# Regions of rows per expert, paced loads and a new order of the attention in a sketched-attention and hash-routed expert kernel

## The chip, the cores and the metric

The kernel runs on one core of a Trainium2 chip. A core has five engines with a queue of instructions each: PE (matrix multiplications; its weight loads are listed apart as PEld), DVE (vector), ACT (scalar), POOL (general) and SP (here only an issuer of DMAs). Each runs its own queue strictly in order, and semaphores between them make one wait for another. DMAs are issued from the queues of SP, ACT and POOL. The metric is the device time of one execution in microseconds.

## The reference

Attention by a sketched polynomial kernel, then a layer of experts chosen by a hash of the token's number:

```python
batch, n_heads, seq, head_dim = (4, 4, 1088, 32); r = 8
def phi(x):
    a = np.einsum('rd,bhsd->bhsr', S1, x)
    b = np.einsum('rd,bhsd->bhsr', S2, x)
    return np.einsum('bhsi,bhsj->bhsij', a, b).reshape(*x.shape[:-1], r * r)
q_p, k_p = (phi(q), phi(k))
kv = np.einsum('bhsf,bhsd->bhfd', k_p, v)
z = np.sum(k_p, axis=2)
num = np.einsum('bhsf,bhfd->bhsd', q_p, kv)
den = np.einsum('bhsf,bhf->bhs', q_p, z)[..., None] + 1e-06
attn = num / den                          # (B, H, S, D) -> x of (B*S, H*D) = (4352, 128)

expert_idx = token_ids * np.int64(2654435761) % np.int64(8)
for e in range(8):                        # w1: (8, 128, 1024), w2: (8, 1024, 128)
    out[expert_idx == e] = np.maximum(x[expert_idx == e] @ w1[e], 0.0) @ w2[e]
```

## The kernel before

Everything is computed in 32-bit floats. The order of the instructions on each engine is written out by hand: the program's order is the order of each engine's queue.

**Attention.** It goes batch by batch (`b` from 0 to 3). A batch has 1024 main rows, held as 128 partitions by 8 rows, and 64 tail rows; the tails of two batches share one tile of 128 partitions. For the main rows of a batch PE transposes k (`turned`, 8 transposes; ACT copies them out of PSUM in two `kT` tiles) and multiplies by the sketch (`side_ab`, 32 small matmuls to a bank `abk`). `first_copied` has ACT copy the first factor, and DVE multiplies the two to 64 features a row (`main_features`, two operations of 128x1024 a side). q goes the same way, but DVE transposes it in blocks of 32x32 (`q_blocks`, two operations), so that its rows come out in another order within blocks of 32. `parted_features`, used for batch 0, gives the second half of a tile to POOL. `kv_products` (64 matmuls, and 8 for the tail) builds kv and, by a column of ones in the tile `va` (`values`), z; `kv_diagonal` copies it out (`m`). `f_turned` has PE transpose the features of q (16 transposes, four copies by ACT), `x_products` multiplies them by `m` in three chunks, and `normalized` has DVE divide by the denominators into the tile `xs`. `keep_busy` is idle matmul work that fills PE's waits near the start.

**Routing.** DVE finds each token's expert (`route_experts`), a scan counts the tokens per expert along the columns (`route_scan`), PE sums the counts over partitions (`route_counts`), and experts are ordered by how many rows they have left (`route_places`, `route_order`). Rows of the first two batches are early, those of the other two late. An expert takes its first 256 early rows as an early group; what is left joins its late rows, and the expert in place r has room for 320 - 7r of those. `route_slots` turns a token's rank into a slot in one array of 35 tiles of 128 rows (16 operations on 34 columns), with a row past the end for a token that found no room; the rows that the block transposes of q have exchanged are put right by one matmul (`route_blocks`, `route_blocks_end`). POOL scatters the finished rows by an indirect DMA each (`scatter_x`, 34 of 128 rows) to `x_rows` in HBM, with the token's number beside each row. `x_rows` was filled with zeros before (L181). Since an empty slot then reads as token 0, `empty_slots` computes on DVE, during expert group 0, which slots are empty (`none`), and `name_rows` ORs this into the rows' numbers (`put`), which makes the last scatter skip them.

**Experts.** There are 16 groups, the 8 early ones of 256 columns and the 8 late ones of 320 to 271. In group g PE does the 8 parts `c` of layer 1 (L922) with those of layer 2 of the group before (L930) in between; ACT and DVE take turns in `evict`. Beside it, at places (g, c) set by `at`, SP fetches the rows of a later chunk (`fetch`, one DMA a chunk), DVE splits them into 16-bit halves and SP turns them by DMA (`turn_in`), and DVE joins the halves (`join_in`), on which layer 1 of that chunk waits. The results go back in the same way (`turn_out`, `join_out`) and are scattered to the output by POOL. Chunks 0 and 1 are turned by PE instead (`bring`). The experts' weights come in 512 KB pieces, w1 and w2: those of places 0 to 3 are issued during the attention, the other four pairs at (0, 3), (1, 3), (2, 3) and (3, 3) (`load_experts`).

**Loads.** SP's queue issues in this order: k0, q0, k1, v0, q1, the tails of k (4 DMAs), v1, the tails of v (4), k2, q2, the fill of `x_rows`, v2, the tails of q (4), k3, q3, v3, four pairs of weights, four fetches. Two tiles each of k, q and v are in turn, so a load waits till the tile two batches back is read. ACT's queue issues the token ids, the main part (L124) first and then the two tails (L127). Nothing else holds a load back.

Of the kernel before, what the change touches and what calls it, by code (L numbers as in the profile page):

```python
# [9 lines left out]
F32 = mybir.dt.float32  # L10
# [20 lines left out]
def kernel(  # L31
# [12 lines left out]
    nc = tc.nc  # L44
# [18 lines left out]
    EB = B - 2  # L63
    CE = TT * T + 1
    GE, GL, GD = 256, 320, 7
# [7 lines left out]
    XW = DM + 4  # L73
    GQ = T // Q
# [32 lines left out]
    tok = const.tile([P, C, 2], I32)  # L107
# [13 lines left out]
    def load_tok():  # L121

        ids = _words(moe_token_ids).rearrange("(b s two) -> b s two", b=B, two=2)
        nc.scalar.dma_start(tok[:, 0:B * T].rearrange("p (b t) two -> p b (t two)", b=B),  # L124
                            ids[:, 0:SM].rearrange("b (p t) two -> p b (t two)", t=T))
        for x in range(TT):
            nc.scalar.dma_start(tok[half_rows(x), B * T:], ids[x::TT, SM:].rearrange("u s two -> s u two"))  # L127

    def load_tail(src, name):

        t = const.tile([P, B // TT, H, D], F32, name=name)
        for b in range(B):
            nc.sync.dma_start(t[half_rows(b), b // TT], src[b, :, SM:, :].rearrange("h p d -> p h d"))
        return t

    def load_main(src, b, tag):
        t = load.tile([P, H, T, D], F32, tag=tag, name=f"{tag}{b}")
        rows = src[b, :, 0:SM, :].rearrange("h (p t) d -> p h t d", t=T)
        if (b, tag) != (0, "k"):
            nc.sync.dma_start(t[:], rows)  # L140
            return t
# [12 lines left out]
    def load_experts(rs, eng=nc.sync, eng_type=ENG.SP):  # L154
# [3 lines left out]
            skip_runtime_bounds_check_because="a count of the experts ahead of one of them is below their number")  # L158
        for r, e in zip(rs, es):
            eng.dma_start(w1[:, r], moe_w1[bass.ds(e, 1)].rearrange("o p f -> p (o f)"))  # L160
            eng.dma_start(w2[:, r], moe_w2[bass.ds(e, 1)].rearrange("o (c p) d -> p (o c) d", p=P))


    k_t.append(load_main(k, 0, "k"))
    load_tok()
    act = const.tile([P, 1], F32)
    nc.scalar.memzero(act[:])
    zeros = const.tile([P, XW], F32)
    nc.scalar.memzero(zeros[:])
# [6 lines left out]
    v_t.append(load_main(v, 1, "v"))  # L176
    v_tail = load_tail(v, "v_tail")
    k_t.append(load_main(k, 2, "k"))
    q_t.append(load_main(q, 2, "q"))
    x_dram = nc.dram_tensor("x_rows", (ST * P + N, XW), F32)  # L180
    nc.sync.dma_start(x_dram[0:ST * P].rearrange("(n p) d -> p n d", p=P),  # L181
                      zeros[:].unsqueeze(1).to_broadcast([P, ST, XW]))
    v_t.append(load_main(v, 2, "v"))
    q_tail = load_tail(q, "q_tail")
    k_t.append(load_main(k, 3, "k"))
    q_t.append(load_main(q, 3, "q"))
    v_t.append(load_main(v, 3, "v"))


    warm = const.tile([P, 1], BF16)  # L190
    G_.memset(warm[:], 1.0)
    ident = const.tile([P, P], F32)
    make_identity(nc, ident[:])
    own_t = const.tile([P, Q], F32)
# [40 lines left out]

    keep_busy(WARM)


    tokens = const.tile([P, C], F32)
    in_blocks = const.tile([P, B, T], F32)  # L240
    block_less = const.tile([P, 1], F32)
    second_half = const.tile([P, 1], F32)
    xs = [const.tile([P, T, XW], F32, name=f"xs{b}") for b in range(B)]
    xs_tail = [const.tile([P, XW], F32, name=f"xs_tail{u}") for u in range(B // TT)]
    first_slot = const.tile([P, 2, E], F32)
    slot_at = const.tile([P, ST], F32)
    caps_of = const.tile([P, E], F32)

    def numbers():

        for t in xs:
            G_.memset(t[:, :, DM + 1:], 0.0)
        for t in xs_tail:
            G_.memset(t[:, DM + 1:], 0.0)
        for cls in range(B // TT):
            iota_of(tokens[:, main_cols(cls)], [[S, TT], [1, T]], cls * TT * S, T)
        tails = tokens[:, T * TT::CE]
        iota_of(tails, [[TT * S, B // TT]], SM, 1)
        G_.memset(second_half[:], 0.0)
        G_.memset(second_half[P // 2:, :], float(S - SP))  # L260
        G_.tensor_tensor(tails, tails, second_half[:].to_broadcast([P, B // TT]), op=OP.add)
        for u in range(B // TT):
            G_.tensor_copy(xs_tail[u][:, DM:DM + 1].bitcast(I32), tokens[:, tail_col(u):tail_col(u) + 1])
        iota_of(in_blocks[:], [[S, B], [Q, GQ], [T * D, Q]], 0, T)
        for j in range(Q):
            G_.memset(block_less[j * D:(j + 1) * D, :], float(j * (T * D - 1)))
        G_.tensor_tensor(in_blocks[:], in_blocks[:], block_less[:].unsqueeze(2).to_broadcast([P, B, T]), op=OP.subtract)
        for b in range(B):
            G_.tensor_copy(xs[b][:, :, DM:DM + 1].bitcast(I32), in_blocks[:, b].unsqueeze(2))
        iota_of(slot_at[:], [[P, ST]], 0, 1)  # L270
        iota_of(caps_of[:], [[-GD, E]], GL)
        iota_of(first_slot[:, 0], [[GE, E]])
        for r in range(E):
            G_.memset(first_slot[:, 1, r:r + 1], float(E * GE + sum(caps[:r]) + (GAP if r == E - 1 else 0)))
# [63 lines left out]
    RB = 14  # L338
    assert N < 1 << RB - 1 and E << RB < 1 << 23
    pos = const.tile([P, C], F32)  # L340
    sidx = const.tile([P, C], I32)
    none = const.tile([P, ST], I32)
    put = const.tile([P, ST], I32)

    def route_experts():
        eid_i = const.tile([P, C], I32, name="eid_i")
        by_class = eid_i[:].rearrange("p (k c) -> p k c", c=CE)
        for lo, hi, src in ((0, TT * T, tok[:, 0:B * T, 0].rearrange("p (k c) -> p k c", k=NC)),
# [886 lines left out]
```

## Time and profile before

| | us |
|---|---|
| median of 3 runs | 195.11 |
| lowest and highest | 192.71, 195.12 |
| the profiled execution | 195.1 |
| its span, first to last instruction | 193.4 |
| first matmul of the experts (L922) | at 61.6 |
| first scatter of rows to `x_rows` | at 33.6 |
| first fetch of rows from `x_rows` issued | at 56.6 |
| last 16 matmuls of the experts (L1120) | at 186.9, 1.95 long |

A row of a timeline has the start, the duration, the engine, the line of the kernel, the operation, output and inputs, the shapes and how many instructions are merged; in brackets stands how long the engine was idle before it and what ended that. SPq and POOLq are the issuing of those engines. In a row of groups the numbers behind the count are the busy time in us and the mean of one in ns. "Issue" as a releaser means that the profile shows nothing that the engine waited for.

### The profile page before, as it was taken

The page shows a single profiled execution, that of the slowest core. Times are in us where ns is not written, and L with a number is a line of the kernel's source. Part 1 is how long each engine was busy: PE and PEld are TensorE (multiplying, and loading weights), DVE is VectorE, ACT ScalarE, POOL GpSimd, SP SyncE. Part 2 cuts the span into 40 slices and gives each one's busy share as a digit, 9 for nine tenths or more (in the row PEclk, how much of TensorE's full clock was granted, in tenths as well). Part 3 has the DMA queues.
Part 4 walks back from the last instruction along what each step waited for, and adds up shares of the span by engine and source line. Part 5 has one row for each costly group of instructions (what it writes and reads, how often), then busy time and mean ns, then how long its engine had stood idle before and what let it go on. Part 6 is the DMA issues. An engine that isn't in the chain of part 4 may idle for free. (4 is left out here: it accounts for less than half of the span.)

```text
span 193.4 us, 4148 instructions
## 1 busy us (share of the span) xinstructions
PE 173.0 (89%) x1512; PEld 141.7 (73%) x1513; DVE 106.0 (55%) x326; ACT 60.9 (31%) x156; POOL 82.4 (43%) x141
## 2 busy tenths in 40 slices
PE   7849789799487899869999999999999999999990
PEld 2637577699487687648888888777777777778990
DVE  3299999897274875143453365263344746424330
ACT  2423546444241313201332332321313313131320
POOL 7736500877777777040440341240412404144762
PEclk9987999999999999978999999999999999999999
DMA  4896999999729634996924325324223183130110
GB/s 107 272 317 170 299 236 236 363 366 365 239 63 220 202 77 94 255 287 110 261 67 93 84 66 111 73 66 97 67 55 81 40 91 90 27 95 28 40 36 28
DMA packets 48069, 28.40 MB, mean 147 GB/s; under 512 B 22116, under 2 KB 45925, under 8 KB 48048
## 3 DMA queue, kind: packets, MB, share of 16 engines
q1 hardware_dynamic: 44736, 23.43, 48.5%
q0 software_dynamic: 2208, 4.53, 7.6%
q10 hardware_dynamic: 1104, 0.17, 0.5%
q8 instruction: 12, 0.20, 0.5%
q14 instruction: 9, 0.07, 0.1%
HBM read 17.42 MB, written 6.96 MB: 126 GB/s over the span
## 5 line engine op out<-in xcount | busy, mean ns | idle before, releaser
L930 PE MATMUL op<-hT,w 128*128 128x256 f32 (+8 forms) x256 | 77.2, 392 | 0.0
L933 POOL DMA_INDIRECT out_dram<-os,put x35 | 34.0, 971 | 78.7 <-DVE put L814 48.5
L760 DVE TENSOR_SCALAR hT<-hp 128x256 f32<-128x256 f32 (+9 forms) x68 | 28.9, 427 | 56.5 <-PE hp L922 46.0
L930 PEld LDWEIGHTS op<-hT,w 128*128 128x128 f32 x256 | 48.0, 192 | 10.9
L758 ACT ACTIVATE hT<-hp 128x256 f32<-128x256 f32 (+9 forms) x68 | 26.4, 390 | 72.7 <-PE hp L922 68.5
L922 PE MATMUL hp<-xT,w 128*128 128x256 f32 x128 | 38.6, 391 | 3.9 <-issue 2.8
L922 PE MATMUL hp<-xT_late,w 128*128 128x320 f32 (+8 forms) x144 | 41.9, 385 | 0.0
L660 POOL DMA_INDIRECT x_rows<-xs,sidx x32 | 31.9, 996 | 20.0 <-DVE den L653 11.4
L922 PEld LDWEIGHTS hp<-xT,w 128*128 128x128 f32 x128 | 24.4, 194 | 8.8 <-issue 3.2
L922 PEld LDWEIGHTS hp<-xT_late,w 128*128 128x128 f32 x144 | 25.4, 190 | 6.8
L626 PE MATMUL fT_ps<-ident,f 128*128 128x128 f32 x64 | 8.4, 279 | 2.1 <-issue 1.9
L575 DVE TENSOR_TENSOR f<-first_of_ab,abq_ps 128x1024 f32<-128x1024 f32 x7 | 8.3, 1217 | 3.5 <-ACT first_of_ab L562 3.5
L833 DVE COPY xh<-xg 128x256 uint16<-128x256 uint16 (+1 forms) x28 | 9.6, 386 | 0.0
L627 ACT COPY fT<-fT_ps 128x512 f32<-128x512 f32 x16 | 8.4, 605 | 2.7 <-PE fT_ps L626 2.7
L626 PEld LDWEIGHTS fT_ps<-ident,f 128*128 128x128 f32 x64 | 6.8, 140 | 3.2 <-issue 2.4
L608 PE MATMUL kv<-va,kp 128*64 128x66 f32 x256 | 8.5, 222 | 0.3 <-ACT both_of_ab L569 0.3
L608 PEld LDWEIGHTS kv<-va,kp 128*64 128x64 f32 x256 | 8.2, 137 | 0.7 <-POOL is_at L401 0.7
L575 DVE TENSOR_TENSOR kp<-first_of_ab,abk_ps 128x1024 f32<-128x1024 f32 x7 | 8.2, 1205 | 0.8 <-ACT first_of_ab L562 0.8
L637 PE MATMUL x_ps<-m,fT 128*64 128x66 f32 x256 | 8.4, 222 | 0.0
L537 PE MATMUL abq_ps<-s_k,qT 128*64 128x64 f32 x128 | 5.6, 237 | 3.2 <-issue 3.0
L637 PEld LDWEIGHTS x_ps<-m,fT 128*64 128x64 f32 x256 | 8.0, 137 | 0.3 <-issue 0.2
L970 ACT COPY half<-op 128x256 uint16<-128x256 uint16 x16 | 5.2, 375 | 7.4 <-PE op L930 7.4
(195 smaller groups left out, 153.5 us busy)
## 6 DMA issues: line engine op xcount, KB each, us to landing
w<-in_moe_w_dram SPq DMA_DIRECT2D x16, 512.0 KB, 7.4
x_rows<-zeros SPq DMA_DIRECT2D x1, 2310.0 KB
q<-in_q_dram SPq DMA_DIRECT2D x4, 512.0 KB, 5.2
v<-in_v_dram SPq DMA_DIRECT2D x4, 512.0 KB
xg<-x_rows SPq DMA_DIRECT2D x13, 129.0 KB, 2.4
k<-in_k_dram SPq DMA_DIRECT2D x3, 512.0 KB, 4.3
xg<-x_rows SPq DMA_DIRECT2D x3, 193.5 KB, 2.6
out_dram<-os,put POOLq DMA_INDIRECT x35, 2.5
```

Of the source, the lines that this page charges most:

```text
L575: eng.tensor_tensor(dst, a[:, r].unsqueeze(3).to_broadcast(shape), ab[:, r].unsqueeze(2).to_broadcast(shape), op=OP.mult)
L608: nc.tensor.matmul(kv[HALVES[x], z], f[:, x], w.rearrange("p h d -> p (h d)"), start=(n == 0 and z == 0), stop=(n == T), skip_group_check= ...
L626: nc.tensor.transpose(p[:, j, z], f[:, (t0 + j) // Q, z, (t0 + j) % Q].rearrange("p h f -> p (h f)"), ident[:])
L627: nc.scalar.copy(fT[:, t0:t0 + 2], p[:])
L637: nc.tensor.matmul(p[x, j, z], fT[:, t0 + j, z, x], m[:, z], start=True, stop=True, skip_group_check=True)
L660: st_ = G_.indirect_dma_start(out=x_dram[:], out_offset=bass.IndirectOffsetOnAxis(ap=sidx[:, c:c + 1], axis=0), in_=row, in_offset=None, b ...
L758: nc.scalar.activation(dst, src, AF.Relu if relu else AF.Copy)
L760: return nc.vector.tensor_scalar(dst, src, 0.0, None, op0=OP.max).ins
L833: nc.vector.tensor_copy(xh[:, x * w:(x + 1) * w].rearrange("p (a b) -> p a b", a=n), xg3[k][:, 0:n].bitcast(U16).rearrange("p a (b two) -> ...
L922: nc.tensor.matmul(hp[:, 0:hi - lo], w1[:, g % E, c * P:(c + 1) * P], x_columns(first_of(g) + lo, first_of(g) + hi), start=True, stop=True)
L930: nc.tensor.matmul(ops[g][:, 0:hi - lo], w2[:, g % E, c], hTs[g][:, c, lo:hi], start=(c == 0), stop=(c == FC - 1))
L933: st_ = nc.gpsimd.indirect_dma_start(out=out[:], out_offset=bass.IndirectOffsetOnAxis(ap=idx, axis=0), in_=src, in_offset=None, bounds_che ...
```

## The change

- **Rows.** `x_rows` gets a region of 256 + 4352 rows per expert, in the experts' order. A token's row there is one sum: its place times the region's length, plus its rank among the expert's rows (`route_rows`); early rows past 256 run on into the part of the late ones. `route_bases`, `route_ranks`, `route_slots` and `empty_slots` go. The early rows' numbers are ready with `route_early`; `route_late` and the block matmul follow for the late ones, in batch 2.
- **Empty rows.** The fill writes rows whose number is too large for the output to be written (`empty_row`), in four DMAs and one for the gap, instead of zeros in one DMA; `name_rows` becomes a copy. It is issued ahead of v1.
- **Fetches.** A chunk that straddles two regions is fetched in several DMAs.
- **Batches** come in the order 0, 2, 1, 3 (`BATCH`), so that each tail tile is loaded by two DMAs instead of four. The tail of the ids has a tile of its own; one half is issued first on ACT, the other by POOL.
- **Room**: 313 - 5r instead of 320 - 7r. The sum is the same, 2364 columns.
- **Paced loads.** `pace` makes a load of SP wait until the third before it has landed. The last four pairs of weights are issued singly, at (0, 2), (0, 6) and then (g, 4) for g from 1 to 6, each after PE's latest matmul of layer 1 at that place.
- **q of the first two batches** is transposed by PE (`side_turned`) with copies by ACT, and its rows keep their order.
- **Order of the attention.** The features of q of batch 0 are all made by DVE; the value tails are copied by ACT and the k tail's features made by DVE instead of POOL. The loop is arranged so that in batch b come, in this order, kv, the transposes of q's features, the products of the next k, x, the products of the next q and the transposes of the k after, while DVE makes the features of k, normalises and then makes those of q.
- The loop for overflowing tokens at the end, which these inputs don't enter, is rewritten for the new rows.

```diff
+    BATCH = [0, 2, 1, 3]
-    GE, GL, GD = 256, 320, 7
+    GE, GL, GD = 256, 313, 5
+    XR = GE + N
...
+        tail(0, nc.scalar)
+        nc.scalar.dma_start(tok[:].rearrange("p (b t) two -> p b (t two)", b=B),
                             ids[:, 0:SM].rearrange("b (p t) two -> p b (t two)", t=T))
+        return lambda: tail(1, nc.gpsimd)
...
+    def pace(ld, ahead=3):
+        if len(paced) >= ahead:
+            tc.add_manual_dep(ld.ins, paced[-ahead].ins.name,
+                              mybir.DependencyInfo(mybir.DependencyClass.Sync, mybir.DependencyReason.DATA), reason="pace")
+        paced.append(ld)
...
-            nc.sync.dma_start(t[:], rows)
+            pace(nc.sync.dma_start(t[:], rows))
...
+        for lo, hi, p in ((0, GE, P), (GE, GE + FL, h)):
+            n = (hi - lo) // p
+            for es in (slice(0, E // 2), slice(E // 2, E)):
+                pace(nc.sync.dma_start(regions[es, lo:hi].rearrange("e (p n) d -> p e (n d)", n=n),
+                                       empty_row[0:p, 0:n].rearrange("p n d -> p (n d)").unsqueeze(1)
+                                       .to_broadcast([p, E // 2, n * XW])))
+        nc.sync.dma_start(x_dram[1 + E * XR:], empty_row[:, 0])
...
+    G_.memset(empty_row[:, :, DM:DM + 1].bitcast(I32), BIG)
+    fill_rows()
+    v_t.append(load_main(v, 1, "v"))
+    q_tail = load_tail(q, "q_tail")
...
+        nc.vector.tensor_tensor(cnt[:, 0, 1], cnt[:, 0, 1], took[:], op=OP.add)
+        nc.vector.scalar_tensor_tensor(base[:], place[:].unsqueeze(1).to_broadcast([P, NC, E]), float(XR), cnt[:, 0],
                                        op0=OP.mult, op1=OP.add)
+    def route_rows(u, dst):
+        rows = seq[:, :, u]
+        nc.vector.tensor_tensor(rows, rows, base[:, u].unsqueeze(2).to_broadcast([P, E, CE]), op=OP.add)
+        nc.vector.tensor_tensor(rows, rows, mask[:, :, u * CE:(u + 1) * CE], op=OP.mult)
+            nc.vector.tensor_reduce(dst, rows.rearrange("p e c -> p c e"), axis=AX.X, op=OP.add)
...
+    kT = side_turned(k_t[0])
     route_experts()
     route_scan()
+    same_in_blocks()
     keep_busy(2)
     abk = side_ab(kT, "abk_ps")
+    cp_of()
+    kp = parted_features(parted_copied(abk), "kp", 2)
+    number_early()
+    number_late()
+    cnt = route_counts()
+    qT = side_turned(q_t[0])
     keep_busy(3)
     va = values(0, nc.scalar.copy)
+    abq = side_ab(qT, "abq_ps", x_bank)
+    firsts = first_copied(flat(abq))
     route_places(cnt)
     route_order()
+    kT = side_turned(k_t[1])
+    f = all_features(firsts, "f", 1)
+    kTt = tail_turned(k_tail, "kTt_ps")
+    for x in range(TT):
+        nc.scalar.copy(va_tails[x][half_rows(x), :, :, 0:D], v_tail[half_rows(x)])
     kv = kv_products(0, kp, va, None, 0, T)
+    abt = tail_products(kTt, "abt_ps")
+    tail_features(kp_tail, first_copied(abt))
+    route_early()
+    fT = f_all(f)
     kv_products(0, kp, va, kv, T)
     m = kv_diagonal(0, kv)
+    abk = side_ab(kT, "abk_ps")
...
+    for b in range(1, B):
+        kv = kv_products(b, kp, va)
+        m = kv_diagonal(b, kv)
+        if b == 1:
+            qT = q_blocks(q_t[2])
+        if b == 2:
+            route_late()
+        fT = f_all(f)
...
+            abk = side_ab(kT, "abk_ps")
+            if b == 2:
+                route_blocks_end(route_blocks(x_bank))
...
+        x_ps = x_all(b)
...
+            kp = all_features(firsts, "kp", 2)
+            abq = side_ab(qT, "abq_ps")
+            firsts = first_copied(flat(abq))
+        if next2:
+            kT = side_turned(k_t[b + 2])
+        x_normalized(b, x_ps)
...
+            f = all_features(firsts, "f", 1)
...
+            lds = load_experts(range(E // 2))
+            for ld in lds[:6]:
+                pace(ld())
+            for k in range(4):
+                fetch(k)
+            for ld in lds[6:]:
+                pace(ld())
...
-    for r in range(E // 2, E):
-        at(r - E // 2, 3, load_experts, range(r, r + 1))
+        ld = later.pop(0)()
+        tc.add_manual_dep(ld.ins, last_mm[0].ins.name,
+                          mybir.DependencyInfo(mybir.DependencyClass.Sync, mybir.DependencyReason.DATA), reason="pace")
+    places = [(0, 2), (0, 6)] + [(g, 4) for g in range(1, E - 1)]
+    for i, (g, c) in enumerate(places):
+        at(g, c, load_next, None if i % 2 else E // 2 + i // 2)
```

More of the change, by code (lines that the diff above doesn't have):

```diff
@@ L247 @@
[L247 to L253, printed above, removed]
-            G_.memset(t[:, DM + 1:], 0.0)
[L255 to L274, printed above, removed]
@@ L462, in route_blocks_end @@
     def route_blocks_end(p):
-        V = nc.vector
         own = spread[:].rearrange("p (n t) i -> p n t i", t=Q)
-        V.tensor_tensor(own, p[:], own_t[:].unsqueeze(1).unsqueeze(3).to_broadcast([P, NC * TT * GQ, Q, Q]), op=OP.mult)
-        V.tensor_reduce(gap[:, 0:NC * TT * T], own.rearrange("p n t i -> p n i t"), axis=AX.X, op=OP.add)
-        for u in range(NC):
-            V.tensor_copy(sidx[:, main_cols(u)], gap[:, u * TT * T:(u + 1) * TT * T])
-    filled = const.tile([P, ST], F32)
@@ L507, in turned @@
+        nc.vector.tensor_tensor(own, p[:], own_t[:].unsqueeze(1).unsqueeze(3).to_broadcast([P, TT * GQ, Q, Q]), op=OP.mult)
+        with nc.allow_low_precision(reason="the numbers of rows are whole"):
+            nc.vector.tensor_reduce(sidx[:, main_cols(1)], own.rearrange("p n t i -> p n i t"), axis=AX.X, op=OP.add)
     def turned(src, g):
@@ new lines, in x_normalized, with x_all @@
+    def x_normalized(b, x_ps, chunks=CHUNKS):
+        for (t0, n), p in zip(chunks, x_ps):
+            normalized(xs[b][:, t0:t0 + n, 0:DM], p, n)
+            for t in range(t0, t0 + n):
+                scatter_x(xs[b][:, t], col_of(b, t))
+    def x_all(b):
+        return [x_products(fT, m, t0, n) for t0, n in CHUNKS]
+    x_ps = x_all(0)
+    qT = side_turned(q_t[1])
+    va_next = values(1, nc.scalar.copy)
+    kp_next = feature_tile(work, "kp", 2)
+    main_features(kp_next, firsts, 0)
@@ L893 @@
             scatter_tail(1)
-        if more:
-            kp, va = kp_next, va_next
-        if b == TT:
-            for k in range(4):
-                fetch(k)
     feats.release()
@@ L1047, with load_next @@
     at(0, 3, bring, 1)
[L1050 to L1052 removed]
     for k in range(4, G):
         at(k - 3, 2, fetch, k)
[L1055 to L1056 removed]
+    later = []
+    def load_next(r):
+        if r is not None:
+            later.extend(load_experts(range(r, r + 1)))
+        ld = later.pop(0)()
[4 more added lines that the diff above has]
+        at(g, c, load_next, None if i % 2 else E // 2 + i // 2)
     for k in range(G):
```

398 lines of the change are left out of this document (159 added, 239 removed).

## The prediction

> **What bounds the kernel now.** I read the page first (busy shares, the 40 slices), then stretches of the span with each engine's busy time, then the timeline where PE is not full.
>
> ```profile
> span 193.4 us, 4148 instructions
> ...
> PE 173.0 (89%) x1512; PEld 141.7 (73%) x1513; DVE 106.0 (55%) x326; ACT 60.9 (31%) x156; POOL 82.4 (43%) x141
> ...
> PE   7849789799487899869999999999999999999990
> ```
> ```profile
> 10.00:20.00 10.00, 7.40 (x138) 6.33 (x139) 9.59 (x21) 2.97 (x7) 4.90 (x7) 0.83 0.90 244
> ```
> ```profile
> 24.90:61.40 36.50, 30.97 (x738) 28.44 (x740) 27.44 (x61) 16.82 (x37) 21.32 (x22) 1.00 0.92 261
> ...
> 66.50:188.90 122.40, 119.16 (x535) 97.23 (x535) 56.48 (x199) 33.44 (x95) 41.81 (x44) 0.99 0.41 95
> ```
>
> The columns of a stretch are its length, then busy time and count of PE, weight loads, DVE, ACT, POOL, then clock, DMA share and GB/s. From 66.5 us on PE is the bound (119.2 of 122.4). Before that nothing is full for long: from 10 to 20 us DVE is (9.59 of 10), with PE's clock at 0.83; from 24.9 to 61.4 PE has 31.0 of 36.5. So the sum goes by three marks on PE: M1, the end of the transposes of batch 0's q features (25.4, the row of 24.98 below); M2, the end of the last x products (61.4); M3, the first matmul of expert group 1 (66.5).
>
> **To M1.**
>
> ```profile
> 8.36 0.17 DVE L350 TENSOR_SCALAR eid_i<-tok 128x2 int32<-128x2 int32 x1 [2.73 <-DMA tok<-in_moe_token_ids_dram]
> ...
> 9.40 2.48 DVE L356 TENSOR_TENSOR_SCAN seq<-keep,mask 128x272 f32<-128x272 f32 x1
> ...
> 12.18 0.17 PE L363 MATMUL cnt<-cp,before 128*128 128x16 bf16 x1 [2.74 <-ACT cp L360]
> ...
> 14.18 1.97 PE L511 MATMUL kT_ps<-ident,k 128*128 128x128 f32 x8
> ...
> 15.94 1.08 PE L234 MATMUL idle<-warm 128*128 128x512 bf16 x3
> ...
> 19.18 1.13 PE L537 MATMUL abk_ps<-s_k,kT 128*64 128x64 f32 x32
> ...
> 24.98 0.44 PE L626 MATMUL fT_ps<-ident,f 128*128 128x128 f32 x2 [1.69 <-issue]
> ```
> ```profile
> tok<-in_moe_token_ids_dram ACTq DMA_DIRECT2D x2, 1.0 KB, 4.3
> ```
> ```profile
> 29.11 1.09 PE L511 MATMUL kT_ps<-ident,k 128*128 128x128 f32 x8
> ```
>
> The tails of the token ids land last, and DVE waits 2.73 us for them. One now goes first on ACT, the other is issued by POOL. How soon a piece issued by POOL lands is not in the trace: with the 4.3 us of ACT's pieces, after an issue near 2 us, it gains 2.1 us, at worst nothing; I take 1.5, nearest to the same small piece. The counting matmul then runs at 10.7 instead of 12.2, and PE idles some 1.9 us before it instead of 2.74; I take it that the slow clock (8 transposes 1.97 instead of 1.09) doesn't follow. Behind it on PE stand 8 new transposes of q (1.1), three keep-busy matmuls (1.1) and the products of q (1.1): 14.0, about as now (14.18), because the q transposes take what the ids gave. From there to M1 PE needs 11.2 us today. Of these go 1.13 (32 products, now behind M1), 1.08 (the keep-busy work, now ahead), 0.9 (the slow clock) and the 1.69 of waiting: 6.4 stay, and I add 0.2 for ACT, which copies the value tails now. M1 is 20.6, 4.8 earlier; bounds 2 (the ids gain nothing, the slow clock stays) and 6 (ids 2.1, no other wait).
>
> **M1 to M2.**
>
> ```profile
> L575 DVE TENSOR_TENSOR f<-first_of_ab,abq_ps 128x1024 f32<-128x1024 f32 x7 | 8.3, 1217 | 3.5 <-ACT first_of_ab L562 3.5
> ...
> L545 DVE STREAM_TRANSPOSE qT<-q 128x512 f32<-128x512 f32 x8 | 5.2, 683 | 0.0
> ```
> ```profile
> L516 ACT COPY kT<-kT_ps 128x512 f32<-128x512 f32 x8 | 4.5, 590 | 5.1 <-PE kT_ps L511 5.1
> ```
> ```profile
> 14.60:17.95 3.35, 3.09 (x33) 2.28 (x33) 2.97 (x13) 1.62 (x4) 1.64 (x4) 0.72 0.53 114
> 20.30:25.55 5.25, 3.10 (x33) 2.35 (x34) 4.80 (x23) 2.67 (x7) 1.91 (x4) 1.00 1.21 288
> ```
>
> In these two stretches DVE does little but routing, 7.8 us. The new routing needs 7 small operations for places and bases, two passes of three over half the columns, four for the late rows and one for the order; at about 0.2 each, the passes about 1.0 each, 4.4. DVE also loses 4 transposes (4 x 0.683 = 2.7) and gets half a feature tile (1.2) and the tail features (half of 1.2 more) from POOL: some 4 less in all, nearly all ahead of M1. ACT gets four copies (4 x 0.59) for the transposes; with 16.8 busy of 36.5 they are free. But M1 to M2 now holds more: PE 31.0 plus the moved products (1.1) plus the second batch's q transposes (1.1) less half of the block matmul (0.2), 33.0; DVE 27.4 plus the late routing (2), about 30. Walking the new order with these prices, PE waits for DVE some 3.5 us: the features of q stand behind the normalising on DVE and the transposes of f behind them (batches 2 and 3, near 42 and 53 us), and the block matmul behind the late rows. That makes 36.5 without any other stall; bounds 33.0 and 40.
>
> ```profile
> q8 instruction: 12, 0.20, 0.5%
> ```
> ```profile
> 0.00:24.95 24.95, 18.44 (x219) 12.71 (x220) 17.61 (x54) 8.94 (x20) 14.41 (x71) 0.93 0.87 234
> ...
> 0.00:51.00 51.00, 40.59 (x727) 32.79 (x728) 39.19 (x99) 22.54 (x49) 27.83 (x85) 0.97 0.99 277
> ```
> ```profile
> 51.12 0.39 PE L537 MATMUL abq_ps<-s_k,qT 128*64 128x64 f32 x5 [2.51 <-issue]
> ```
>
> The "issue" waits in mid-row (1.69, 2.51) are, I think, PE without instructions: they come 439 and 1455 records into PE's stream, 1016 apart, and queue q8 moved 12 packets in 0.20 MB, 16 KB each, while PE and its loads have 1512 + 1513 records; so a packet is about 256 of them, and 1016 is about four packets. The DMA engines' share was 0.87 to 0.99 till then. The new kernel crosses as many such borders, and paced loads leave the engines nearly as full. Bounds 0 and 4.2; I take 2.2, half of it, since PE then also waits for DVE and the two overlap. M1 to M2 is 38.7 (36.0 now) and M2 is 59.3: 2.1 earlier.
> The Trainium skill ("Runtime: NRT & Kernel Launch", Instruction fetch mechanics) says that blocks of 256 instructions are fetched while the last ones run, and that crossing a border is mostly hidden; by that rule this term is 0 and the time 2.2 lower. The trace doesn't bear it out (2.51 us).
>
> **Scatters, fill and loads, at no cost.**
>
> ```profile
> 33.62 1.21 POOL L660 DMA_INDIRECT x_rows<-xs,sidx  x1 [10.46 <-DVE den L653]
> ```
> ```profile
> 15.00:17.50 2.50, 2.24 (x16) 1.43 (x16) 2.16 (x11) 1.62 (x4) 1.27 (x3) 0.71 0.51 83
> ...
> 25.00:30.00 5.00, 5.00 (x116) 4.53 (x116) 4.93 (x10) 2.52 (x6) 0.00 (x0) 1.00 1.26 230
> ```
>
> By the same walk the first scatter comes near 25 instead of 33.6, since early rows no longer pass the block matmul, and POOL's numbering, which stands before it, is over by then. The 17 early ones end near 50, so the fetches on SP land before PE asks for them. The fill (2.4 MB, four paced pieces and one more) now stands ahead of v of the second batch on SP. At 230 GB/s it takes 10.5 us from 12.5, and v lands near 25, when ACT wants it: no slack, each us more is one on M2. Each paced load waits for the third before it; behind it on SP stand tails, fills and later fetches. With 1.5 MB under way the engines have work meanwhile.
>
> **M2 to M3.**
>
> ```profile
> 59.34 2.09 PE L637 MATMUL x_ps<-m,fT 128*64 128x66 f32 x64
> ...
> 63.35 0.29 DVE L655 TENSOR_TENSOR xs_tail<-x_ps,den 128x128 f32<-128x128 f32 x1
> ...
> 63.88 0.66 ACT L758 ACTIVATE hT<-hp 128x256 f32<-128x256 f32 x2 [4.05 <-PE xp L824]
> ...
> 64.27 0.73 DVE L478 TENSOR_TENSOR below_f<-slot_at,first_slot 128x560 f32<-128x560 f32 x1
> ...
> 66.54 0.67 PE L922 MATMUL hp<-xT,w 128*128 128x256 f32 x2 [0.23 <-ACT hT L758]
> ```
>
> The first evictions start when DVE has normalised the last rows (63.64), 2.2 us behind M2, and that chain stays. DVE's search for empty slots, which begins with the 0.73 at 64.27 between evictions, falls away, so the waiting banks empty faster: 0.4 earlier; bounds 0 and 1.
>
> **M3 to the end.**
>
> ```profile
> 76.00 0.37 SPq L161 DMA_DIRECT2D w<-in_moe_w_dram  x1
> ...
> 76.47 1.21 SPq L835 DMA_TRANSPOSE xh_turned<-xh  x1
> ...
> 80.27 0.59 PE L922 MATMUL hp<-xT,w 128*128 128x256 f32 x2
> ...
> 80.70 0.59 PE L930 MATMUL op<-hT,w 128*128 128x256 f32 x2
> ...
> 83.50 0.51 DVE L840 COPY xT<-xh_turned 128x256 uint16<-128x256 uint16 x2 [3.90 <-DMA xh_turned<-xh]
> ...
> 84.11 0.67 PE L922 MATMUL hp<-xT,w 128*128 128x256 f32 x2 [2.82 <-issue]
> ...
> 85.35 1.06 PE L922 MATMUL hp<-xT,w 128*128 128x256 f32 x2
> ...
> 88.47 0.59 PE L922 MATMUL hp<-xT,w 128*128 128x256 f32 x2
> ```
>
> The transfer that turns group 3's rows, issued at 76.47 behind two weight loads (the second at 76.00), lands 7 us later. PE idles 2.82 and then runs at half speed: from 84.11 to 88.47 it starts six such pairs, which at 0.43 a pair (80.27 to 80.70) need 2.6, so 1.75 are lost. Of the 3.24 us that PE idles in the whole stretch this is nearly all. Now one load of 512 KB goes per group, released by PE's own matmul, and with half the bytes ahead the turning should land in 4 to 5 us, within a group (16 x 0.43 = 6.9). I take 4.8 (2.82 + 1.75 + 0.2); bounds 0 and 5. The fetches in pieces (up to three for one per late group) lengthen SP's queue by about a us per group; it has nothing else new to do there: 0. Sizes 313 to 278 instead of 320 to 271 sum to the same 2364 columns.
>
> **The sum.** -2.1 - 0.4 - 4.8 = -7.3 from the profiled run's 195.1 (span 193.4 and 1.7 around it), which is the median of the runs: 187.8.
>
> **Rivals.** (1) PE's waits for instructions vanish under pacing: 185.6. For it: from 66.5 on, at a DMA share of 0.41, PE idles 3.24 us, 2.82 of them over rows; against: the early loads stay as dense. (2) The attention gets no shorter, DVE's longer second part eats what M1 gains: 187.8 + 2.1 = 189.9. For it: DVE's 30 us there. (3) The turned rows come late all the same, behind the single load: + 4.8, 192.6. Against: no later group pays today. (4) Clock: PE makes 16 more transposes, and the clock falls twice more as it did from 10 to 20 us, where 0.17 of 10 us, 1.7, went: 191.2. Against: from 24.9 to 61.4 the clock was 1.00 over the transposes of three batches. The Trainium skill ("TensorE: Matmul & The Clock Gate", Part 4) says that transposes don't count as work for the clock gate; by that rule this rival happens. The trace speaks against it (1.00). (5) Slower: the fill starves v of the second batch. At the 83 GB/s of 15 to 17.5 us it takes 29 us, v lands 18 us late and all moves by that: 205.8. It turns slower than now once the fill takes 18 us, below 135 GB/s. Against: 230 where most of the present fill runs.
>
> **How the numbers follow.** Forecast 0.36, (1) 0.16, (2) 0.18, (3) 0.13, (4) 0.07, (5) 0.10. The likeliest, 187.8, has 185 to 191 of its own. The range 183.5 to 193.5 takes in all but (5) and a little of (1). A measurement of this kernel tells about 2% from no change, so the line is at 191.2. Faster: forecast, (1), (2) and half of (4), 0.735, less 0.045 that spills over: 0.69. Within 2%: (3), half of (4), the spill and a mild (5), 0.22. Slower 0.09.
>
> **What would show it.** First scatter near 25 us; M1 near 20.6; M2 near 59, with DVE before PE's transposes of f; no gap at the third group and clock 1.00 there. I am wrong if ACT waits for v of the second batch, if the clock dips before 20 us, or if PE's long "issue" gaps grow.

## The result, and the profile after

| | before | changed |
|---|---|---|
| median, us | 195.12 | 189.25 |
| lowest and highest, us | 192.71, 195.14 | 188.01, 189.57 |
| profiled execution, its span | 195.1, 193.4 | 189.09, 187.4 |
| end of batch 0's transposes of q features (M1) | 25.4 | 18.3 |
| end of the last x products (M2) | 61.4 | 60.7 |
| first matmul of group 1 (M3) | 66.5 | 65.3 |
| from M3 to the end of the span | 126.9 | 122.1 |

The changed kernel is faster: ratio 0.971, 95% interval 0.964 to 0.979. A ratio, here and below, is taken over the faster executions of each kernel (those within about 1.5% of its fastest), so it can differ from that of the medians. First the page (the span, PE's busy share, the slices of PE and of its clock):

```profile
span 187.4 us, 4151 instructions
...
PE 171.6 (92%) x1526; PEld 142.2 (76%) x1526; DVE 95.9 (51%) x289; ACT 63.0 (34%) x160; POOL 78.5 (42%) x125
...
PE   7789809997979999999999999999999999999990
...
PEclk9999975999999999999999999999999999999998
```

PE did as much work as before (171.6 against 173.0 us) in 6 us less. The hole of before in slice 17 (counted from 0; 82 to 87 us) is gone; there is a new one in slice 5 (23.4 to 28.1 us), and the clock falls in slices 5 and 6. The timeline of PE there, and of what it waits for:

```profile
9.90 0.17 PE L384 MATMUL cnt<-cp,before 128*128 128x16 bf16 x1 [1.34 <-ACT cp L379]
...
16.34 1.97 PE L575 MATMUL fT_ps<-ident,f 128*128 128x128 f32 x16
...
21.48 1.09 PE L460 MATMUL kT_ps<-ident,q 128*128 128x128 f32 x8
27.85 0.66 PE L471 MATMUL qTt_ps<-ident,q_tail 128*128 128x128 f32 x2 [5.28 <-DMA q_tail<-in_q_dram]
28.44 1.98 PE L486 MATMUL abq_ps<-s_k,kT 128*64 128x64 f32 x32
30.34 1.97 PE L460 MATMUL kT_ps<-ident,k 128*128 128x128 f32 x8
...
44.01 1.87 PE L557 MATMUL kv<-va,kp 128*64 128x66 f32 x57 [0.99 <-issue]
...
56.41 2.23 PE L575 MATMUL fT_ps<-ident,f 128*128 128x128 f32 x16 [1.58 <-DVE f L524]
58.57 2.10 PE L586 MATMUL x_ps<-m,fT 128*64 128x66 f32 x64
...
65.76 0.59 PE L920 MATMUL op<-hT,w 128*128 128x256 f32 x2
```
```profile
11.87 6.29 SPq L207 DMA_DIRECT2D x_rows<-empty_row  x4
18.20 1.11 SPq L210 DMA_DIRECT2D x_rows<-empty_row  x1
19.41 2.04 SPq L159 DMA_DIRECT2D v<-in_v_dram  x1
21.50 2.26 SPq L151 DMA_DIRECT2D q_tail<-in_q_dram  x2
```
```profile
27.04 1.05 ACT L541 COPY va<-v 128x1024 f32<-128x1024 f32 x1 [3.80 <-DMA v<-in_v_dram]
```

PE has transposed batch 0's q features by 18.3 us and runs out of work at 22.6, but SP is busy until 19.3 with issuing the fill (2.2 us of that is the pacing's wait for an earlier piece), so v of the second batch is issued at 19.4 and the tails of q at 21.5. PE waits 5.28 us for the tails, ACT 3.80 for v, and the products behind take 1.98 us instead of 1.17 (at full clock, in a run below). The stretches (length, busy time and count of PE, weight loads, DVE, ACT, POOL, then clock, DMA share and GB/s) say the same:

```profile
18.30:60.70 42.40, 34.24 (x770) 31.38 (x770) 27.69 (x61) 18.16 (x40) 21.89 (x23) 0.92 0.82 238
20.00:30.00 10.00, 4.72 (x94) 4.11 (x90) 4.78 (x11) 2.58 (x5) 3.39 (x4) 0.80 1.00 265
66.00:187.00 121.00, 116.61 (x533) 95.59 (x531) 52.99 (x182) 33.66 (x95) 41.78 (x44) 1.00 0.46 103
```

In 20 to 30 us PE is busy for 4.72 with the DMA engines full (share 1.00). From 66 us on the clock is 1.00, and PE works 116.6 of the 117.0 us up to the end of its last matmul at 183.0. (M3 itself is the pair of matmuls ahead of the row of 65.76, one step of 0.43 earlier.) DVE's writing of the first rows of x, and POOL's scatters, the first and the last of the early ones:

```profile
21.72 0.56 DVE L604 TENSOR_TENSOR xs<-x_ps,den 128x384 f32<-128x384 f32 x1
...
25.70 1.11 POOL L609 DMA_INDIRECT x_rows<-xs,sidx  x1 [8.60 <-DVE xs L604]
...
52.75 0.98 POOL L609 DMA_INDIRECT x_rows<-xs_tail,sidx  x1 [0.30 <-DVE den L602]
```

And the way of group 3's rows, where PE stood still before: a load of weights and the turning on SP, DVE's joining of the halves, PE's first matmuls of the group:

```profile
72.92 0.35 SPq L180 DMA_DIRECT2D w<-in_moe_w_dram  x1
73.37 1.21 SPq L800 DMA_TRANSPOSE xh_turned<-xh  x1
...
78.86 0.51 DVE L805 COPY xT<-xh_turned 128x256 uint16<-128x256 uint16 x2 [1.25 <-DMA xh_turned<-xh]
...
79.48 0.67 PE L912 MATMUL hp<-xT,w 128*128 128x256 f32 x2 [0.17 <-issue]
```

### The profile page after: what moved, and what is told of

It reads as the page before. It is cut to its first block, busy times and chain, and to the rows that moved or that the text cites. A ratio compares the mean times of both kernels' runs of the same rounds, so it can differ in the third digit from the quotient of the medians.

```text
span 187.4 us, 4151 instructions
## 1 busy us (share of the span) xinstructions
PE 171.6 (92%) x1526; PEld 142.2 (76%) x1526; DVE 95.9 (51%) x289; ACT 63.0 (34%) x160; POOL 78.5 (42%) x125
## 5 line engine op out<-in xcount | busy, mean ns | idle before, releaser
L920 PE MATMUL op<-hT,w 128*128 128x256 f32 (+8 forms) x256 | 76.4, 389 | 0.0
L923 POOL DMA_INDIRECT out_dram<-os,put x35 | 34.2, 977 | 74.6 <-DVE put L779 44.2
L920 PEld LDWEIGHTS op<-hT,w 128*128 128x128 f32 x256 | 47.5, 190 | 10.5
L912 PE MATMUL hp<-xT_late,w 128*128 128x313 f32 (+8 forms) x144 | 42.0, 386 | 0.2 <-DVE xT_late L805 0.2
L609 POOL DMA_INDIRECT x_rows<-xs,sidx x32 | 31.4, 982 | 24.4 <-DVE xs L604 8.6
L912 PE MATMUL hp<-xT,w 128*128 128x256 f32 x128 | 37.0, 380 | 0.3 <-issue 0.2
L912 PEld LDWEIGHTS hp<-xT_late,w 128*128 128x128 f32 x144 | 25.4, 190 | 7.2 <-issue 0.6
L524 DVE TENSOR_TENSOR f<-first_of_ab,abq_ps 128x1024 f32<-128x1024 f32 x8 | 9.4, 1214 | 5.8 <-ACT first_of_ab L511 5.8
L465 ACT COPY kT<-kT_ps 128x512 f32<-128x512 f32 x12 | 6.6, 588 | 5.4 <-PE kT_ps L460 5.4
L981 DVE COPY os<-turned 128x256 uint16<-128x256 uint16 (+1 forms) x26 | 7.2, 315 | 0.9 <-DMA turned<-half 0.7
```

Of the source, the lines that this page charges most:

```text
L524: eng.tensor_tensor(dst, a[:, r].unsqueeze(3).to_broadcast(shape), ab[:, r].unsqueeze(2).to_broadcast(shape), op=OP.mult)
L609: st_ = G_.indirect_dma_start(out=x_dram[:], out_offset=bass.IndirectOffsetOnAxis(ap=sidx[:, c:c + 1], axis=0), in_=row, in_offset=None, b ...
L912: last_mm[0] = nc.tensor.matmul(hp[:, 0:hi - lo], w1[:, g % E, c * P:(c + 1) * P], x_columns(first_of(g) + lo, first_of(g) + hi), start=Tr ...
L920: nc.tensor.matmul(ops[g][:, 0:hi - lo], w2[:, g % E, c], hTs[g][:, c, lo:hi], start=(c == 0), stop=(c == FC - 1))
L923: st_ = nc.gpsimd.indirect_dma_start(out=out[:], out_offset=bass.IndirectOffsetOnAxis(ap=idx, axis=0), in_=src, in_offset=None, bounds_che ...
```

## Experiments

Two kinds of chips came up. On one, as where the result above was measured, the kernel before takes 195 us. On four others it takes 222, so mainly ratios to the kernel before on the same chip are compared there, and traces up to about 30 us, where they still agree with the ones above within half a us. None of the ratios on these four is clear of the 2% that count as no change, and the unedited kernel before was not traced there. The runs are ordered by question.

**Is it the place of the fill that makes PE wait?** Three edits of the order on SP, each against the changed kernel:

```diff
 # fill_late: the fill behind q of the third batch
-    fill_rows()
     v_t.append(load_main(v, 1, "v"))
     q_tail = load_tail(q, "q_tail")
     k_t.append(load_main(k, 2, "k"))
     q_t.append(load_main(q, 2, "q"))
+    fill_rows()
```

> Edit: the changed kernel with its loads in another order on SP: v and the two tails of q, k and the second q ahead of the loads that fill the rows with empty ones, the second v behind them. The changed kernel: 189.25 us; TensorE idle 5.28 before the product with the first q tail (at 27.85) and at clock 0.80 in 20 to 30 us. Theory, the order: the tails of q are late only because the fill stands ahead of them; in the other order they land some 5 us earlier, the gap goes and the clock stays at 1.00 until 30 us, and the rows are still full before the first scatter (25.7): the last x product (60.67) comes 3 to 6 us earlier, 183 to 186. Rival, full transfers: 3 MB and more must go through the same 16 engines by then in any order, so that what comes earlier for TensorE is late for the first scatter of rows (which waits for the fill until 30 or later): the scatters end about 5 us later than 53.7, the fetch of the first rows is late for TensorE, and the time stays 188 to 190.

Measured: 186.83 us median, ratio 0.957 (0.953 to 0.961) on a chip where the kernel before takes 194.79. Its profiled execution (188.75, span 187.0) was the longest of its five. PE, then SP, then POOL:

```profile
22.55 0.38 PE L471 MATMUL qTt_ps<-ident,q_tail 128*128 128x128 f32 x2
22.95 1.17 PE L486 MATMUL abq_ps<-s_k,kT 128*64 128x64 f32 x32
...
36.60 1.90 PE L460 MATMUL kT_ps<-ident,k 128*128 128x128 f32 x8 [2.46 <-DMA k<-in_k_dram]
...
53.96 2.10 PE L586 MATMUL x_ps<-m,fT 128*64 128x66 f32 x64
58.92 0.41 PE L789 MATMUL xp<-ident,xg 128*128 128x128 f32 x2 [2.87 <-DMA xg<-x_rows]
...
59.81 3.09 PE L912 MATMUL hp<-xT,w 128*128 128x256 f32 x8
...
65.70 0.59 PE L920 MATMUL op<-hT,w 128*128 128x256 f32 x2
```
```profile
13.02 2.36 SPq L151 DMA_DIRECT2D q_tail<-in_q_dram  x2
...
17.25 8.02 SPq L207 DMA_DIRECT2D x_rows<-empty_row  x4
...
56.39 1.92 SPq L770 DMA_DIRECT2D xg<-x_rows  x4
```
```profile
33.26 1.11 POOL L609 DMA_INDIRECT x_rows<-xs,sidx  x1 [15.99 <-DMA x_rows<-empty_row]
...
54.02 0.98 POOL L609 DMA_INDIRECT x_rows<-xs_tail,sidx  x1 [0.30 <-issue]
```

The order was the cause: the wait of 5.28 us is gone, and M2 comes at 56.1 instead of 60.7, though PE now waits 2.46 us for the next k, which stands behind the fill. But the rival was right on what is late next. The first scatter now waits for the fill until 33.26 (25.70 in the changed kernel); 17 scatters at one per 1.28 us end at 55.0, the fetch is issued at 56.39, and PE waits 2.87 us for it. This fetch hardly moves between the kernels (56.6 before, 56.19 changed, 56.39 here), so PE can begin on its rows at 58.92, 1.75 us ahead of the changed kernel's 60.67, and no earlier. The eight matmuls behind that take 3.09 us instead of 2.00, and the row that was at 65.76 stands at 65.70: in this execution the whole 4.6 us are given back by M3. The other four took 186.2 to 187.0 at a mean clock of 0.987 to 0.990 (0.981 here), so a little of it stays; that the difference is this slow stretch is likely but was not seen, as they have no trace. Of 5 us the reordering brought some 2: 186.83 against 189.25, on two chips whose kernels before are 0.3 apart, or against 188.6 on this chip for the changed kernel with one small edit on POOL (below).

The same kernel on one of the slower chips:

> Edit: the fill is issued behind v of the second batch, the tails of q, the third k and the third q. Theory 'order': all that PE and ACT want before 30 us lands by then, no gap above 1 us before the second x products, clock 1.00 throughout; the last x products end near 54 instead of 60.7; the fill lands near 30, the first scatter waits for it (30 instead of 25.7), the 17 early scatters need 21.8 us and end near 52 to 53, and the fetch is in time or a us late; time 189.2 - 5 = 183 to 185. Theory 'full engines': the scatters, 4 us later, now set the fetch and with it the experts' start; time 187 to 190.

219.46 us, ratio 0.977 (0.968 to 0.985). No wait for the tails either (they are transposed at 22.22), and the first scatter at 31.71.

With only v and the tails of q ahead of the fill, on the same chip:

> Edit: in the changed kernel v of the second batch and the tails of q are issued ahead of the fill, the fill ahead of the third k. Theory 'order': PE's gap of 5.3 us before the q tails (22.5 to 27.85) and the slow clock after it (two rows of about 1.9 us where 1.1 is usual) come from the fill standing ahead of these loads on SP; both go, but the third k, now the first load behind the fill, lands near 28 and PE waits for it some 2 to 3 us; time 189.2 - 4 = 185, between 183 and 187. Theory 'full engines': the DMA engines are full until 28 us whatever stands first, and PE or the scatters wait for the same bytes elsewhere; time 188 to 190.

223.05 us, ratio 1.013 (1.008 to 1.019). The wait for the tails is gone, but PE then waits 5.66 us for the next k, which now stands behind the fill: the hole moves by one load. With k ahead of the fill too, and q of the third batch behind it:

> Edit: the changed kernel with v, the tails of q and k of the second batch ahead of the fill, and q of the third batch (that is, the second load of q that stood ahead of the fill in the run before this one) behind it. With that load ahead too, the first scatter of rows waited for the fill until 33.26 us, 17 scatters at one per 1.28 us ended at 55.0, the last product of x ended at 56.1, and TensorE waited 2.87 us for the first fetch; 186.83 us. Theory, the scatters: the first starts 512 KB earlier (about 2 us at 265 GB/s), at 31, the fetch lands at 57 and TensorE waits 1 us or none, while q, later by the bytes of the fill, holds TensorE up by about 1 us at 35: 184 to 186. Rival, full transfers: whatever is put ahead, something else is late by as much: q holds TensorE up by 3 us or more near 33 us, the last product of x moves to 58 or later: 187 to 189.

214.38 us, ratio 0.976 (0.959 to 0.992), on another of the slower chips. The first scatter starts at 30.92, as the theory had it, and from M1 to 30 us PE waits no longer than 0.5 us; what this is worth at M3 can't be read there, since from 33 us on PE waits again and again on "issue". That it is the best order is open.

**Does pacing make the wait?** The wait of each load for the third before it was taken out (`if False:` in `pace`):

> Edit: no load waits for the third before it (the weights' waits for PE's matmuls stay). If pacing is what removed PE's waits without a releaser (4.2 us before, 1.0 after), they come back: two or three of 1.5 to 2.5 us, time 190 to 192. If they went because PE crosses the borders of its instructions at other moments, time 188 to 190 and no new ones. A third possibility: without pacing the loads of v and of q's tails are queued sooner, and the gap of 5.3 us gets shorter; time 186 to 188.

222.86 us, ratio 1.015 (1.007 to 1.023) on a slower chip. PE waits 5.48 us for the tails of q, as with pacing (5.33 in the unedited kernel on such a chip), and the first scatter waits for the fill until 26.39. SP comes to v at 18.99 (19.69 in the unedited kernel there), so pacing is hardly what delays them; the order is. Whether pacing removes waits on "issue" can't be read on such a chip: there are 21.4 us of them without it and 20.7 with it.

**What are the early transposes of q by PE worth?** DVE does them again (`q_blocks` for `side_turned` at batches 0 and 1):

> Edit: the changed kernel with q of the first two batches transposed by VectorE in blocks of 32, as in the kernel before. Their rows then stand in another order within 128, which is not put right, so the rows of x of these two batches (and of the output) are exchanged; the amount of work is otherwise the same. VectorE gets 4 transposes (0.65 each), TensorE loses 16 (2.1 us) and ScalarE 4 copies. Theory, the counting matmul: TensorE's transposes stand in the way between the counting and the first features; VectorE's stand beside it: the early transposes of f end 1 us later to 0.5 earlier than 18.3, and since TensorE then waits for the tails of q near 27.9 in any case, the time is 188.5 to 190. Rival, VectorE is the early bound: each transpose moves it later, the early transposes of f end 2 us or more later (20.5) and the first scatter too, with 190 to 192.

219.4 us on a slower chip, ratio 1.004 (0.997 to 1.010). Its PE, up to the wait:

```profile
12.22 1.97 PE L486 MATMUL abq_ps<-s_k,qT 128*64 128x64 f32 x32 [1.46 <-DVE qT L494]
...
19.48 1.97 PE L575 MATMUL fT_ps<-ident,f 128*128 128x128 f32 x16
...
27.98 0.41 PE L471 MATMUL qTt_ps<-ident,q_tail 128*128 128x128 f32 x2 [3.30 <-DMA q_tail<-in_q_dram]
```

PE waits 1.46 us for DVE, then runs at half speed (1.97 for products that took 1.15), and M1 is 21.4 instead of 18.3, so the rival's "2 us or more" holds. Yet the transposes of the tails start at 27.98 as against 27.85 in the changed kernel (28.31 on such a chip). So 3.1 us at M1 are worth 0.1 us or nothing behind the wait: what the change gains before 22 us is absorbed by the late loads. Nor does the first scatter move (25.71). Here it follows DVE's writing of its rows, which ends at 25.42, by 0.29 us; in the changed kernel these rows are ready at 22.28 and 3.4 us pass. There it is not x that holds it up; the releaser that the trace names (DVE) had long been done, and the run without pacing names the fill.

**What made the stall at group 3?** The kernel before, with the weights alone changed:

```diff
-    for r in range(E // 2, E):
-        at(r - E // 2, 3, load_experts, range(r, r + 1))
+    places = [(0, 2), (0, 6)] + [(g, 4) for g in range(1, E - 1)]
+    for i, (g, c) in enumerate(places):
+        at(g, c, load_next, None if i % 2 else E // 2 + i // 2)
```

> Edit: the kernel before with one part of the change alone: the last four pairs of weights issued singly, each behind TensorE's latest matmul, at the changed kernel's places. The kernel before: TensorE idle 2.82 us at 84.11 and at half speed until 88.5, because the turned rows of group 3 land 7 us after their issue behind two weight loads. Theory, the weights: the stall and the half speed go, 4 to 5 us less: 190 to 191.5. Rival, the rest of the queues (the fetches and the search for empty slots on VectorE, which this kernel still has): the rows are turned as late as before: 194 to 195.5.

216.67 us, ratio 0.984 (0.969 to 0.999), on a slower chip. From group 1 on PE shows no gap that waits for a group's rows, although DVE still searches for empty slots; the one gap left is 1.15 us in the last group, which the runs on these chips have in some form. That the unedited kernel before has the stall on such a chip was not seen. The reverse, pairs in the changed kernel, three times on slower chips:

> Edit: the last four pairs of weights are issued as before the change, w1 and w2 together at (0,3), (1,3), (2,3), (3,3), without waiting for PE. Theory of the prediction: the turned rows of chunk 3 land late behind two loads and PE's gap (2.8 us) and half clock (1.8 us) come back; time 189.2 + 4.6 = 194, at least 191.5. Rival: what ended the gap is that DVE, free of the search for empty slots, turns its rows earlier; time 188.5 to 190.

> Edit: the changed kernel with the last four pairs of weights issued as in the kernel before (both of a pair at part 3 of groups 0 to 3, not held back). The changed kernel: 189.25 us, no gap at group 3, last matmul 121.4 us after the first of group 1. Theory, the weights: the gap of 2.8 us and the half speed come back, 192 to 194. Rival, the gap belongs to the old kernel's other queues: 188.5 to 190.

> Edit: as in the two runs with pairs of weights before this one (the changed kernel, the last four pairs issued both at once and not held back), which ran on chips where the kernel before took 222 us and TensorE was short of instructions until 95 us. There the rows behind a pair landed 5.5 to 6.4 us after their issue, and TensorE lost 0.82 and 0.96 us at one group, with the clock at 1.00; the kernel before with single weights lost nothing. On a chip where the kernel before takes 195: theory, the weights alone make the stall of the kernel before: 2.5 to 3 us of idling and the half speed behind it come back at group 3, 121.4 becomes 125 to 126 us from the first matmul of group 1 to the end, and the time is 192.5 to 194. Rival, the weights make it together with the rest of the old order: a gap of 0.5 to 1.2 and no slow clock, 189 to 190.5.

225.38 us (no ratio), 219.6 (1.002, 0.995 to 1.009) and 225.25 (1.017, 0.997 to 1.037). (The 121.4 us that the expectations name start 0.7 us after M3; by the same matmul in both kernels it is 122.1.) The row of PE's timeline in the second of them (0.96 and 0.89 in the other two):

```profile
123.10 0.67 PE L912 MATMUL hp<-xT,w 128*128 128x256 f32 x2 [0.82 <-ACT half L960]
```

With pairs one gap comes back ahead of an early group (group 5, not group 3), 0.82 to 0.96 us in all three, with no slow clock behind it. With single loads there is none at those groups, in the old kernel as in the new; on such a chip the unedited changed kernel has one of 0.75 us later, at the late groups. The gap and clock that the rival of the last of them names ("0.5 to 1.2 and no slow clock") are what was seen. The turned rows of groups 3 and 5 land 5.5 to 6.8 us after their issue with pairs, and at most 4.7 after it in the unedited changed kernel on such a chip. So pairs slow the turning and make a small stall in the changed kernel, but no run here shows that they alone made the 2.82 us and the half speed of before, and no pairs were run on the faster kind of chip.

The two traces from the faster chips show that more than the pairs is in it. Counted from M3, group 3's rows land 3.4 us earlier than before (78.86 less 65.33, as against 83.50 less 66.54). Of that, 1.5 us are the shorter transfer (5.5 us instead of 7.0) and 0.8 that SP issues the turning sooner after DVE has split the rows, with one load ahead of it instead of two. The other 1.1 us are DVE's: it has split the rows 7.8 us after M3 (73.09) instead of 8.9 (75.40). In the kernel before, the search for empty slots stands on DVE from 64.27 to 70.5, and the split of group 2's rows comes in the midst of it (69.75; 65.00 in the changed kernel). So the rival of the first run with pairs, that DVE is free of the search, has a share that no run tested alone.

**Why did the scan get shorter?** In the kernel before, the scan of the choices took 2.48 us from 9.40; after, 0.72. Before, it ran beside POOL's product for the features of k. POOL's half was put ahead of the copy of the choices again:

```diff
+    copied = parted_copied(abk)
     cp_of()
-    kp = parted_features(parted_copied(abk), "kp", 2)
+    kp = parted_features(copied, "kp", 2)
```

> Edit: the changed kernel, but GpSimd's first half of the features of k is put ahead of the copy of the choices, as in the kernel before, so that GpSimd works beside VectorE's scan again. The changed kernel: scan of the choices 0.72 us from 8.87, beside an idle GpSimd; the kernel before: 2.48 from 9.40, beside GpSimd's product for k. Theory, shared access: a VectorE operation is slowed while GpSimd works: the scan takes 2.2 to 2.6 again, the counting matmul comes 1.5 to 1.9 later than 9.90, the last early transposes end at 19.8 to 20.3 instead of 18.3, and the time is the same within 1 us, because the stall before 27.85 then takes up less. Rival, the scan is short for its own sake (its data or its form): 0.7 again, and nothing else moves.

188.6 us, ratio 0.967 (0.960 to 0.975), beside fill_late. Rows of POOL and DVE, first of the kernel before, then of the changed one, then of this run:

```profile
9.35 1.95 POOL L575 TENSOR_TENSOR kp<-both_of_ab 128x1024 f32<-128x1024 f32 x1 [0.97 <-ACT both_of_ab L569]
```
```profile
10.37 1.95 POOL L524 TENSOR_TENSOR kp<-both_of_ab 128x1024 f32<-128x1024 f32 x1 [3.80 <-ACT counts L387]
```
```profile
7.75 0.18 DVE L367 TENSOR_SCALAR eid_i<-tok 128x32 int32<-128x32 int32 x1 [2.20 <-DMA tok<-in_moe_token_ids_dram]
7.84 0.16 DVE L369 TENSOR_SCALAR eid_i<-tok_tail 128x2 int32<-128x2 int32 x1
...
8.87 0.72 DVE L375 TENSOR_TENSOR_SCAN seq<-keep,mask 128x272 f32<-128x272 f32 x1
...
9.89 0.23 DVE L308 COPY in_same<-in_block 128x128 f32<-128x128 f32 x1
...
11.46 0.89 DVE L393 TENSOR_SCALAR took<-counts 128x8 f32<-128x8 f32 x1
```
```profile
9.74 2.10 POOL L524 TENSOR_TENSOR kp<-both_of_ab 128x1024 f32<-128x1024 f32 x1 [3.21 <-ACT both_of_ab L518]
```
```profile
9.38 0.72 DVE L375 TENSOR_TENSOR_SCAN seq<-keep,mask 128x272 f32<-128x272 f32 x1
...
10.39 1.53 DVE L308 COPY in_same<-in_block 128x128 f32<-128x128 f32 x1
...
12.98 0.20 DVE L393 TENSOR_SCALAR took<-counts 128x8 f32<-128x8 f32 x1
```

The number expected for the scan missed: it stays 0.72, because POOL's operation begins at 9.74, after it. But the copy that starts at 10.39 now takes 1.53 us instead of 0.23 and ends at 11.92, where POOL's ends (11.84); the 0.89 of the small operation that stood beside POOL in the changed kernel is 0.20 here. So some DVE operations that start while POOL works wait for POOL's end; the scan, which started first (9.38 against 9.74), went through in 0.72. The Trainium skill ("SBUF — State Buffer", SBUF: two separate sides) says that DVE and POOL share a pair of ports, which a POOL operation, or a DVE operation of certain kinds, holds until its end if it starts first; the trace agrees (0.23 against 1.53). That this made the 2.48 of before fits: POOL began 0.05 us ahead of the scan and ended at 11.30, and 0.72 more is 12.02, where the scan ended at 11.88. But the scan was not seen slowed again. The time stayed within 1 us, as expected, since PE then waits for the tails of q all the same (until 28.00).

**Is the change worth as much on the slower chips?** The changed kernel, unedited:

> No edit: the changed kernel itself, for a chip like those of most runs here, where the kernel before takes 222 us and TensorE waits for instructions from about 32 to 95 us. Theory, the waits for instructions are the bound there until 95 us and the change takes none away: what it gains (7 us less at the end of the attention and in group 3) is in part lost in these waits, ratio 0.99 to 1.02, like the variants with the fill ahead of v (1.002 to 1.017). Rival, the change is worth the same 5 to 6 us wherever it runs: ratio 0.97 to 0.98, and the variants above 1.00 are worse for what they edit. Should the chip be one where the kernel before takes 195: 188 to 190 again.

The medians are 223.47 us against 222.42, the ratio is 1.017 (1.008 to 1.026): no gain is seen there, and a loss of a per cent or two is likely but not clear. PE's longest waits in all:

```profile
PE kv L557 <- issue: 10.7, 14, 1.1
PE fT_ps L575 <- issue: 6.2, 2, 5.0
PE qTt_ps L471 <- DMA q_tail<-in_q_dram: 5.3, 1, 5.3
PE hp L912 <- issue: 3.8, 3, 1.6
```

The columns are the waiting group, what it waited for, the sum in us, the times and the longest. PE waits on "issue" for 20.7 us (10.7 + 6.2 + 3.8) instead of 1.2, mostly about 1 us at a time with a few matmuls between, all before 100 us; the rest of the 35 us by which its span is longer (222.5 against 187.4) is mostly lost clock in between (0.79 from 31 to 96 us). The kernel before with single weights has 18.0 us of such waits on such a chip, so most of them are not the change's doing. That the gain of the first part of the kernel drowns in them fits, but wasn't shown; nor was it traced why fill_late (0.977) and fill_between (0.976) do better than the changed kernel there.

## Why the prediction was right, and where not

187.8 was forecast, 189.25 came, within the range and on the right side. That the total came so close owes something to luck: two terms were off by 2.3 and 3.7 us, in opposite directions. By its steps:

- **To M1: mis-sized, -7.1 instead of -4.8.** The ids gained 0.5 us (8.36 to 7.84) where 1.5 was taken, since DVE now waits for their main part (7.75), which goes behind a tail on ACT's queue; but the scan took 1.76 less, which the sum didn't have, and the counting matmul came at 9.90 (10.7 expected). From there to M1 it took 8.4 us instead of 9.9: the three rows put in took 2.8 instead of 3.3 (9.90 to 12.69), two short waits of PE for ACT in the kernel before (0.26 and 0.46) went too, and the 0.2 added for ACT wasn't needed. That the slow clock wouldn't follow held (1.00 up to 20 us).
- **M1 to M2: the step that failed, 42.4 instead of 38.7.** PE is busy for 34.2 (33.0 expected; half clock, 0.50 from 27.9 to 32.7, costs some 2 us, more than the difference) and idles 8.2 (5.7 expected). Of the idle time 5.28 is the wait for the tails of q. "v lands near 25, when ACT wants it: no slack" named the place, and it was not free: ACT had waited since 23.2, and v came at 27.0, so that one of the prediction's own signs of being wrong, ACT waiting for v, came true. The sum costed the fill by its bytes and looked at v alone; the tails stand behind v on SP, and PE meets them first. It is rival (5) in a mild form, and with M1 earlier it costs more, as q_blocks shows from the other side. Of the waits that the sum did have, "issue" was 0.99 (2.2 taken) and DVE's features 1.58 and a little (3.5 taken); some of both is hidden by the new wait.
- **Scatters.** The first was near 25 (25.70) as said, but held up by the fill, as far as the runs tell, rather than by x (ready at 22.3). The early ones ended at 53.7 instead of 50, and the fetch, issued at 56.2 (56.6 before), still landed in time.
- **M2 to M3: right**, 4.7 us (5.1 before), the 0.4 forecast.
- **M3 to the end: right**, 4.8 us less, as forecast. The stall and the slow clock behind it are gone: PE idles 0.4 us to its last matmul instead of 3.2, and is busy 117.1 instead of 119.2. Its cause, that pairs of weights hold up the turned rows, is half shown: single loads leave no stall at the early groups, pairs a smaller one. The rows land 5.5 us after their issue, not 4 to 5, and just in time (PE's gap is 0.17); about a third of what they gain comes from DVE's earlier split, which the prediction didn't count.
- **Rivals.** (1) was nearly so for the waits on "issue" on this chip (1.2 us left of 4.2), not for the time, and no run shows that pacing is the reason; (2) came nearly true in its outcome (M2 only 0.7 us earlier), but by the loads, not by DVE. (3) and (4) did not happen: the clock fell, but behind a wait of 5.28 us and not over the transposes.

So the miss of 1.3 us (the profiled execution took 189.09) is M1's surplus of 2.3 and an M1-to-M2 part 3.7 too long.

## What to carry to other kernels

A load placed ahead on an issuing queue delays everything behind it there: when an early part gets faster, walk the queue down to the first transfer that it will now meet, not only to the next one. With the DMA engines full, as here from 20 to 30 us, moving one transfer mainly chose who waits: taking 5 us of wait from one place gave some 2 us, since the scatters and the fetch behind them were the next limit. Two milestones of PE and the idle time between them, term by term, show which gains are kept and which a wait absorbs.

## What was not expected of the hardware

- A DVE copy of 128x128 took 1.53 us beside a POOL operation, 0.23 without.
- Four chips ran the kernel before in 222 us and not 195. In the changed kernel there, PE waited 20.7 us on "issue" before 96 us (1.2 here), and the gain of 2.9% was not seen (ratio 1.017, by the medians 1.005). Why is open.
